# Linear attention twice on one core: mask constants and iotas at other steps, four natural tiles in an idle accumulator, half a weight chunk on another queue

## The chip, the cores and the metric

The kernel runs on one core of a Trainium2 chip. The core has five engines with instruction streams of their own, tied together by semaphores only: TensorE (PE in the profile, PEld for its weight loads), VectorE (DVE), ScalarE (ACT), GpSimd (POOL) and SyncE (SP), which here only issues DMAs. The metric is the device time of one execution in microseconds.

## The reference

Two independent linear-attention blocks A and B with the same shapes; their outputs are put side by side.

```python
# for each block: x (1, 2048, 640), wqkv (640, 1920), wo (640, 640), 32 heads of 20
q, k, v = split(x @ wqkv)                            # per head
phi = lambda t: where(t > 0, t + 1, exp(t)) + 1e-6
pq, pk = phi(q), phi(k)
kv  = einsum("bhsd,bhse->bhde", pk, v)               # summed over all 2048 rows
z   = einsum("bhsd->bhd", pk)
o   = einsum("bhqd,bhde->bhqe", pq, kv) / (einsum("bhqd,bhd->bhq", pq, z) + 1e-6)
out = o.reshape(1, 2048, 640) @ wo
```

All in float32.

## The kernel before, in words

**Accuracy.** A float32 product is made of three faster ones: each operand is split into a high part (a rounded copy, line 198, on ACT) and a low part (operand minus high, line 195, on DVE), and the kernel sums high·high, low·high and high·low. A name that ends in h or l is such a part: `wh`, `wl` of a weight chunk, `kah`, `kal` and `ksh`, `ksl` of transposed x, `xnh`, `xnl` of natural x, `pkh`, `pkl` of phi(k).

**Tiling.** x has 32 tiles of 128 rows (16 of A, 16 of B) and 5 chunks of 128 columns. Every tile comes in twice from DRAM: transposed ("t", for k = x·wk) and natural ("n", for the sums). Both go into the five buffers `xr` (`load_x`, line 418), issued on SP.

**Stages.** (1) The head (lines 1106 to 1171): the first three tiles' chunks and the chunks of wk arrive in small DMAs and are split at once; seven dummy matmuls on `psi` run meanwhile. Then `first_chunk` does chunk 0 of tiles 0 to 2, with the left half of the weight chunk's columns first and the right half after it, and the steps ("c", n, c) do chunk c of tile n (`plain`, line 606), up to tile 5. Chunks 0 and 1 of wk use `wh`, `wl`; the later ones use `wfh`, `wfl`. (2) From tile 6 on, k is computed for two tiles at a time by steps ("p", p, product), a Strassen-like form (line 350) with sums of weight blocks (the jobs `f1`, `f2`, lines 866 to 874, on DVE) and sums of x (the jobs `s1` to `s6`, line 459); its parts are added up in `ko` by the jobs `q` (line 357, on DVE). (3) phi in four jobs per tile: `exp`, `relu`, `mix` (line 565), and the split `ph` (line 577, ACT) and `pl` (line 581, DVE). z is summed by an accumulating DMA on POOL's queue (`zs`, `zd<-ek`). (4) The sums G = phi(k)ᵀ·x over groups of four tiles, steps ("H" or "G", group, slice), lines 205 to 207 into `psg`, whose results DVE adds into the accumulator `gacc` of 5 x 640 columns (line 651; the first group is copied, line 649). The jobs `nh` and `nl` split natural x for them. (5) kv from G (line 788), then the denominators, the q products (`psq`) and the output, from about 291 us to the end.

**What sets the order.** The steps of TensorE are listed once, then shifted by the table `MOVED`. Every job of the other engines has a place, a step plus a number from the table `SHIFT`; a job's instructions on all its engines, its DMAs included, are issued at that place. `perform` sorts both lists and issues everything in that order; each engine then runs its own instructions strictly in order. The loads of wk of block B ("ld", "k", 1, c), the stores ("st", pair, part) of split x to DRAM (lines 270 to 274) and the loads of x all share SP's queue.

**Constants.** `constants` makes the three masks used from stage 5 on: three iotas on POOL and six DVE operations (lines 313 to 321), all at step ("c", 4, 2).

Of the kernel before, what the change touches and what calls it, by code (L numbers as in the profile page):

```python
# [14 lines left out]
H = 32  # L15
# [15 lines left out]
    ('fdl', 'k', 1, 4): 4.77, ('fdl', 'k', 1, 8): 1.97, ('fdl', 'm', 0, 1): -0.43, ('fdl', 'm', 0, 2): 1.2, ('fdl',  # L31
# [8 lines left out]
    ('gacc', 0, 3): 0.36, ('gacc', 0, 6): 1.73, ('gacc', 1, 3): 0.64, ('gacc', 1, 5): 1.74, ('gacc', 2, 1): 2.89,  # L40
    ('gacc', 2, 3): 0.28, ('gacc', 3, 0): 0.42, ('gacc', 3, 1): 2.86, ('gacc', 3, 2): 2.99, ('gacc', 3, 3): 3.83,
    ('gacc', 3, 5): 2.14, ('gacc', 3, 6): 1.96, ('gacc', 4, 0): 0.75, ('gacc', 4, 4): 2.17, ('gacc', 4, 5): 4.46,
    ('gacc', 5, 0): 0.6, ('gacc', 5, 3): 1.28, ('gacc', 5, 5): 0.51, ('gacc', 5, 6): 1.36, ('gacc', 6, 2): 0.82,
    ('gacc', 6, 4): 0.59, ('gacc', 7, 0): 0.31, ('gacc', 7, 1): 0.04, ('gacc', 7, 2): 2.56, ('gacc', 7, 4): 0.07,
    ('gacc', 7, 5): 0.78, ('gacc', 7, 6): 2.69, ('iota', 0): 0.8, ('kt', 0): 0.53, ('kt', 1): 1.13, ('kt', 5): 4.11,
    ('kvh', 0): 1.2, ('kvh', 1): 5.05, ('kvh', 4): 1.1, ('kvl', 1): 2.02, ('kvl', 3): 2.08, ('kvl', 5): -0.64,
    ('ld', 'k', 1, 1): -0.06, ('ld', 'k', 1, 2): -2.17, ('ld', 'k', 1, 3): -8.75, ('ld', 'k', 1, 4): -3.84, ('ld',
    'm', 0, 0): 1.22, ('ld', 'm', 0, 1): 0.8, ('ld', 'm', 0, 2): 1.54, ('ld', 'm', 0, 3): -0.03, ('ld', 'm', 0, 4):
    -0.19, ('mc', 4, 1): 0.69, ('mix', 0): -0.53, ('mix', 10): 0.15, ('mix', 11): 0.24, ('mix', 12): 0.49, ('mix',
    13): 7.61, ('mix', 14): 4.05, ('mix', 15): 0.17, ('mix', 17): 1.76, ('mix', 19): 1.66, ('mix', 20): 0.31,  # L50
# [87 lines left out]
def tile_linear_attn_pair(ctx: ExitStack, tc: tile.TileContext, ins, out: bass.AP):  # L138
# [171 lines left out]
    def constants():  # L310
        ij = base.tile([P, P], I32, name="ij", tag="kvt", bufs=3)
        nc.gpsimd.iota(ij, pattern=[[1, P]], base=0, channel_multiplier=-1)
# [1275 lines left out]
```

## Time and profile before

| | us |
|---|---|
| runs | 571.79, 572.67, 573.43 (median 572.67) |
| profiled execution | 572.12 |
| its span on the core | 570.3 |
| outside the span | 1.8 |
| PE busy | 564.0 (99%) |
| DVE busy | 438.6 (77%) |
| ACT busy | 334.6 (59%) |
| POOL busy | 84.3 (15%) |

The granted TensorE clock was 1.0 over the span. A timeline row gives start, duration, engine, line, operation, the tile written and the tiles read, and in brackets the idle time of that engine just before and what ended it; "SPq" or "ACTq" is a DMA issue, whose duration is that of issuing. Matmuls overlap in the pipeline, so their spacing is read from start to start.

### The profile page before, as it was taken

The numbers are of one execution on the slowest core, as the hardware profiler recorded it, in microseconds if no ns is written. First come the engines' busy times: TensorE is split into PE (matmuls) and PEld (weight loads), VectorE is DVE, ScalarE is ACT, GpSimd is POOL, SyncE is SP. The second block draws the span as 40 slices with busy tenths as digits, with TensorE's granted clock in tenths as the row PEclk, the third lists the DMA queues.
The fourth block names the chain that finished last, engine by engine and source line by source line (L and its number), as shares of the span: only waits on it lengthen the run. The fifth ranks groups of instructions, "written<-read, shape, count | busy, mean of one in ns | idle before, by whom it ended". The sixth has DMA issues, their size and how long they took to land.

```text
span 570.3 us, 9067 instructions
## 1 busy us (share of the span) xinstructions
PE 564.0 (99%) x3243; PEld 513.8 (90%) x3243; DVE 438.6 (77%) x729; ACT 334.6 (59%) x625; POOL 84.3 (15%) x141
## 2 busy tenths in 40 slices
PE   8999999999999999999999999999999999999997
PEld 6989989898999898989888899898989989898997
DVE  6888698886584878788745799977798786768792
ACT  6863667664575775656736665746556464644551
POOL 0121132411011212143100103220012201001010
PEclk9999999999999999999999999999999999999999
DMA  8777689999985786998998977762455994122022
GB/s 285 192 206 201 180 208 333 269 326 363 340 185 130 190 238 114 376 236 260 334 273 279 328 231 251 260 193 95 131 197 170 393 366 140 48 66 92 1 93 92
DMA packets 71700, 123.58 MB, mean 217 GB/s; under 512 B 9000, under 2 KB 33960, under 8 KB 71656
## 3 DMA queue, kind: packets, MB, share of 16 engines
q1 hardware_dynamic: 59352, 83.29, 44.7%
q0 software_dynamic: 12160, 39.66, 25.1%
q8 instruction: 25, 0.41, 0.3%
q14 instruction: 19, 0.16, 0.1%
q10 hardware_dynamic: 144, 0.07, 0.0%
HBM read 73.62 MB, written 49.37 MB: 216 GB/s over the span
## 4 chain that ended last, share of the span: by engine, by line
PE 89%; DVE 5%; DMA 4%; issue 1%; ACT 1%; SPq 0%; POOL 0%; POOLq 0%; DVEq 0%; ACTq 0%
PE pa L350 21%; PE pe L350 11%; PE psq L205 8%; PE psq L207 8%; PE psq L206 8%; PE psg L206 7%; PE psg L207 7%; PE psg L205 7%; PE psb L350 6%; PE pskv L788 2%; PE psk L606 2%; DMA wst<-in_B_wk 1%; DMA zd<-ek 1%; DVE xnl L195 1%; DMA x<-in_A_xt_tiles 1%
## 5 line engine op out<-in xcount | busy, mean ns | idle before, releaser
L205 PE MATMUL psq<-xqh,wqh 128*128 128x512 f32 x200 | 78.4, 392 | 0.0
L207 PE MATMUL psq<-xqh,wql 128*128 128x512 f32 x200 | 78.0, 390 | 0.0
L206 PE MATMUL psq<-xql,wqh 128*128 128x512 f32 x200 | 77.9, 389 | 0.0
L207 PE MATMUL psg<-pkh,xnl 128*128 128x512 f32 x160 | 62.8, 392 | 0.3 <-DVE xnl L195 0.3
L206 PE MATMUL psg<-pkl,xnh 128*128 128x512 f32 x160 | 62.8, 393 | 0.0
L205 PE MATMUL psg<-pkh,xnh 128*128 128x512 f32 x160 | 62.8, 393 | 0.0
L354 ACT ACTIVATE o<-pa 128x320 f32<-128x320 f32 x64 | 27.9, 439 | 45.8 <-PE pa L350 45.6
L958 DVE SCALAR_TENSOR_TENSOR pq<-eq,rq 128x512 f32<-128x512 f32 x40 | 27.6, 690 | 27.7 <-ACT rq L957 27.7
L573 POOL DMA_DIRECT2D zd<-ek x30 | 26.1, 870 | 136.1 <-DVE ek L565 59.9
L207 PEld LDWEIGHTS psq<-xqh,wql 128*128 128x128 f32 x200 | 37.5, 188 | 7.9
L956 ACT ACTIVATE eq<-psq 128x512 f32<-128x512 f32 x40 | 23.9, 597 | 34.9 <-PE psq L207 32.6
L354 ACT ACTIVATE ko<-pa 128x320 f32<-128x320 f32 x52 | 22.5, 434 | 37.3 <-PE pa L350 37.1
L206 PEld LDWEIGHTS psq<-xql,wqh 128*128 128x128 f32 x200 | 37.6, 188 | 7.2
L205 PEld LDWEIGHTS psq<-xqh,wqh 128*128 128x128 f32 x200 | 37.6, 188 | 7.2
L207 PEld LDWEIGHTS psg<-pkh,xnl 128*128 128x128 f32 x160 | 30.0, 188 | 7.0 <-DVE xnl L195 0.7
L206 PEld LDWEIGHTS psg<-pkl,xnh 128*128 128x128 f32 x160 | 30.0, 188 | 6.3 <-DVE pkl L581 1.0
L205 PEld LDWEIGHTS psg<-pkh,xnh 128*128 128x128 f32 x160 | 30.1, 188 | 5.3 <-DVE kvt L795 0.2
L577 ACT ACTIVATE pkh<-ek,epst 128x640 fp32r<-128x640 f32 x32 | 26.3, 831 | 8.4 <-DVE ek L565 8.3
L651 DVE TENSOR_TENSOR gacc<-psg,gacc 128x512 f32<-128x512 f32 (+2 forms) x42 | 26.0, 628 | 6.2 <-PE psg L207 5.9
L581 DVE SCALAR_TENSOR_TENSOR pkl<-ek,pkh 128x640 fp32r<-128x640 f32 x32 | 26.0, 820 | 5.2 <-ACT pkh L577 5.2
L195 DVE TENSOR_TENSOR xnl<-xn,xnh 128x640 fp32r<-128x640 f32 x32 | 25.8, 818 | 5.4 <-ACT xnh L485 5.1
L565 DVE SCALAR_TENSOR_TENSOR ek<-ek,ko 128x640 f32<-128x640 f32 x32 | 26.2, 820 | 4.6 <-ACT ko L562 3.3
(208 smaller groups left out, 1679.5 us busy)
## 6 DMA issues: line engine op xcount, KB each, us to landing
zd<-ek POOLq DMA_DIRECT2D x32, 320.0 KB, 5.7
out<-o POOLq DMA_DIRECT2D x28, 320.0 KB, 3.9
xql<-xd SPq DMA_DIRECT2D x24, 256.0 KB, 4.0
xn<-in_A_x SPq DMA_DIRECT2D x16, 320.0 KB, 5.5
xt<-in_B_xt_tiles SPq DMA_DIRECT2D x16, 320.0 KB, 5.3
xn<-in_B_x SPq DMA_DIRECT2D x16, 320.0 KB, 5.6
xqs<-in_A_xt SPq DMA_DIRECT2D x20, 256.0 KB, 6.3
xqs<-in_B_xt SPq DMA_DIRECT2D x20, 256.0 KB, 4.2
```

The lines of the kernel that those rows point to most:

```text
L195: nc.vector.tensor_tensor(lo, src, f32(hi), op=OP.subtract)
L205: nc.tensor.matmul(o, whi, xhi, start=first, stop=False)
L206: nc.tensor.matmul(o, whi, xlo, start=False, stop=False)
L207: nc.tensor.matmul(o, wlo, xhi, start=False, stop=last)
L350: nc.tensor.matmul(o, x, y, start=start and m == r == 0, stop=m == len(terms) - 1 and r == 2, skip_group_check=True)
L354: nc.scalar.activation(x, y, AF.Copy)
L565: nc.vector.scalar_tensor_tensor(ek[n], ek[n], 1.0, rk[n], op0=OP.min, op1=OP.add)
L573: nc.gpsimd.dma_start(zacc[b], e, accum_op=OP.add)
L577: nc.scalar.activation(pk[n][0], ek[n], AF.Identity, bias=epst)
L581: nc.vector.scalar_tensor_tensor(lo, ek[n], EPS, f32(hi), op0=OP.add, op1=OP.subtract)
L651: nc.vector.tensor_tensor(o, x, o, op=OP.add)
L958: nc.vector.scalar_tensor_tensor(pq[u][:, c, :], e, 1.0, r, op0=OP.min, op1=OP.add)
```

## The change

Four edits, and both tables have other numbers.

1. `constants` is cut in two. The three iotas (`counts`) stand at ("p", 3, 0), the six DVE operations at ("p", 4, 5); before, all stood at ("c", 4, 2). The iotas' three buffers are held in between.
2. Natural x of tiles 0 to 3 is loaded into `gacc[0][:, n]`, the accumulator of block A, which holds nothing until the first group's sums are copied into it. Those four loads no longer take an `xr` buffer.
3. The right half of wk's chunk 0 is issued from ACT's queue, right after its x load, and no longer from SP behind x of tiles 1 and 2.
4. Chunk 1 of tiles 0 to 2: the products with the weight's high part are done for all three tiles first, and the products with its low part after them.

```diff
@@ load_x
-        x = xr[kind, n] = kx[0].tile([P, D], F32, name=f"x{kind}", tag="xr", bufs=5)
+        if kind == "n" and n < 4:
+            if n == 0:
+                gacc[0] = base.tile([P, NC, D], F32, name="gacc", tag="gacc", bufs=1)
+            x = xr[kind, n] = gacc[0][:, n]
+        else:
+            x = xr[kind, n] = kx[0].tile([P, D], F32, name=f"x{kind}", tag="xr", bufs=5)
@@ plain
-        for i, j in ((0, 0), (1, 0), (0, 1)):
+        for i, j in ((0, 0), (1, 0), (0, 1))[2 * (c == 1 and n in first):]:
@@ head
     nc.sync.dma_start(t[:, :HF], ins[0]["wk"][:P, :HF])
+    nc.scalar.dma_start(t[:, HF:], ins[0]["wk"][:P, HF:])
     part(1, 0, 3)
-    nc.sync.dma_start(t[:, HF:], ins[0]["wk"][:P, HF:])
@@ first_chunk, at its end
+        for n in first:
+            for i in range(2):
+                for h in range(2):
+                    plain_mm(n, 1, i, 0, h)
@@ jobs
-    job(("constants",), ("c", 4, 2), constants)
+    job(("counts",), ("p", 3, 0), counts)
+    job(("constants",), ("p", 4, 5), constants, after=[("counts",)])
@@ SHIFT, one entry of many
-    ('nl', 0): 0.1, ('nl', 1): 2.6,
+    ('nl', 0): -0.75,
```

The lines behind the table stand up to 20 lower in the changed kernel (line 195 is 177 there, 606 is 598).

TensorE in chunk 1 of tiles 0, 1, 2 (its weight parts are `wh`, `wl`; x of tile 0 is `kah`, `kal`, of tile 1 `ksh`, `ksl`, of tile 2 again `kah`, `kal`; x2 are the two column halves). Before:

```order
L606 MATMUL psk<-wh,kah 128x320 x2
L606 MATMUL psk<-wh,kal 128x320 x2
L606 MATMUL psk<-wl,kah 128x320 x2
L606 MATMUL psk<-wh,ksh 128x320 x2
L606 MATMUL psk<-wh,ksl 128x320 x2
L606 MATMUL psk<-wl,ksh 128x320 x2
```

After:

```order
L598 MATMUL psk<-wh,kah 128x320 x2
L598 MATMUL psk<-wh,kal 128x320 x2
L598 MATMUL psk<-wh,ksh 128x320 x2
L598 MATMUL psk<-wh,ksl 128x320 x2
L598 MATMUL psk<-wh,kah 128x320 x2
L598 MATMUL psk<-wh,kal 128x320 x2
L598 MATMUL psk<-wl,kah 128x320 x2
```

The first matmul that reads `wl` stood behind four others of the chunk and now stands behind twelve.

VectorE at the first sums (28 to 35 us before): `pkl` and `xnl` are the low parts that the sums read, `ek<-ek,ko` is `mix`, `ij`, `same` and `mask` are the constants. Before:

```order
L581 SCALAR_TENSOR_TENSOR pkl<-ek,pkh 128x640
L313 TENSOR_SCALAR ij<-ij 128x128
L314 TENSOR_SCALAR same<-ij 128x128
L320 TENSOR_SCALAR mask_438<-v_437 128x120
L321 SCALAR_TENSOR_TENSOR mask_438<-v_437,mask_438 128x120
L320 TENSOR_SCALAR mask_443<-v_442 128x80
L321 SCALAR_TENSOR_TENSOR mask_443<-v_442,mask_443 128x80
L565 SCALAR_TENSOR_TENSOR ek<-ek,ko 128x640
L195 TENSOR_TENSOR wfl_448<-t_267,wfh_447 128x320
L195 TENSOR_TENSOR xnl<-xn,xnh 128x640 x2
L581 SCALAR_TENSOR_TENSOR pkl<-ek,pkh 128x640
```

After (the `xnl<-gacc` are those of tiles 1, 2 and, in the last row, 3):

```order
L177 TENSOR_TENSOR xnl<-gacc,xnh 128x640 x2
L177 TENSOR_TENSOR kal<-xt,kah 128x128
L858 TENSOR_TENSOR t_398<-wst 128x320
L859 TENSOR_TENSOR wst<-wst 128x320
L177 TENSOR_TENSOR ksl<-xt,ksh 128x256
L865 TENSOR_TENSOR t_398<-wst 128x320
L866 TENSOR_TENSOR t_422<-wst,t_398 128x320
L177 TENSOR_TENSOR wfl_418<-t_259,wfh_417 128x320
L557 SCALAR_TENSOR_TENSOR ek<-ek,ko 128x640
L573 SCALAR_TENSOR_TENSOR pkl<-ek,pkh 128x640 x2
L177 TENSOR_TENSOR xnl<-gacc,xnh 128x640
```

The constants are gone from here, and `xnl` of tile 1, which stood behind them beside that of tile 3, now stands nine rows ahead of the last `pkl`.

VectorE in the second group's sums (66 us on before), behind the two `pkl` of tiles 6 and 7: `t` and `wst` are block sums of wk (`f1`), `sx` sums of x, `gacc` the additions. Before:

```order
L581 SCALAR_TENSOR_TENSOR pkl<-ek,pkh 128x640 x2
L459 TENSOR_TENSOR sx<-xt 128x256
L459 TENSOR_TENSOR sx<-sx,xt 128x256
L866 TENSOR_TENSOR t_909<-wst 128x320
L867 TENSOR_TENSOR wst<-wst 128x320
L565 SCALAR_TENSOR_TENSOR ek<-ek,ko 128x640
L651 TENSOR_TENSOR gacc<-psg,gacc 128x512
```

After:

```order
L573 SCALAR_TENSOR_TENSOR pkl<-ek,pkh 128x640 x2
L302 TENSOR_SCALAR ij<-ij 128x128
L303 TENSOR_SCALAR same<-ij 128x128
L307 TENSOR_SCALAR mask_884<-ij 128x120
L308 SCALAR_TENSOR_TENSOR mask_884<-ij,mask_884 128x120
L307 TENSOR_SCALAR mask_887<-ij 128x80
L308 SCALAR_TENSOR_TENSOR mask_887<-ij,mask_887 128x80
L858 TENSOR_TENSOR t_890<-wst 128x320
L859 TENSOR_TENSOR wst<-wst 128x320
L451 TENSOR_TENSOR sx<-xt 128x256
L451 TENSOR_TENSOR sx<-sx,xt 128x256
```

The six operations of the constants stand here now, ahead of the block sums of wk and of the second group's `gacc` additions.

More of the change, by code (lines that the diff above doesn't have):

```diff
@@ L19 @@
 SHIFT = {
[3 rows of a table removed]
-    6): 1.78, ('c5', 8): 1.02, ('constants',): 1.46, ('exp', 0): 2.17, ('exp', 10): 0.04, ('exp', 11): 0.73, ('exp',
-    13): 3.23, ('exp', 14): 0.41, ('exp', 15): 0.95, ('exp', 16): 0.91, ('exp', 18): -0.02, ('exp', 20): -0.96,
-    ('exp', 22): 1.7, ('exp', 25): 0.96, ('exp', 28): 1.07, ('exp', 29): 0.86, ('exp', 3): 4.78, ('exp', 4): 0.2,
[5 rows of a table removed]
-    ('fdl', 'k', 1, 4): 4.77, ('fdl', 'k', 1, 8): 1.97, ('fdl', 'm', 0, 1): -0.43, ('fdl', 'm', 0, 2): 1.2, ('fdl',
[8 rows of a table removed]
-    ('gacc', 0, 3): 0.36, ('gacc', 0, 6): 1.73, ('gacc', 1, 3): 0.64, ('gacc', 1, 5): 1.74, ('gacc', 2, 1): 2.89,
@@ L41 @@
[L41 to L50, printed above, removed]
@@ L51 @@
-    ('mix', 23): 0.53, ('mix', 24): -0.1, ('mix', 26): 0.21, ('mix', 29): 2.2, ('mix', 3): -0.55, ('mix', 4): 7.31,
[20 rows of a table removed]
-    ('relu', 1): 0.33, ('relu', 10): 1.37, ('relu', 11): 0.09, ('relu', 13): 1.06, ('relu', 14): 1.59, ('relu', 17):
-    0.14, ('relu', 2): 0.27, ('relu', 21): 4.46, ('relu', 25): 2.55, ('relu', 28): 1.48, ('relu', 30): 3.49,
[19 rows of a table removed]
-    1.07, ('woh', 4): -0.51, ('wol', 0): 0.5, ('wol', 3): 0.03, ('wol', 4): 0.03, ('wqh', 1): 2.01, ('wqh', 3):
[2 rows of a table removed]
[3 rows of a table added]
+    0): 2.55, ('exp', 11): 0.74, ('exp', 13): 3.23, ('exp', 14): 0.41, ('exp', 15): 0.95, ('exp', 16): 0.91, ('exp',
@@ new lines @@
+    18): -0.02, ('exp', 20): -0.96, ('exp', 22): 1.7, ('exp', 25): 0.96, ('exp', 28): 1.07, ('exp', 29): 0.86,
+    ('exp', 3): 4.78, ('exp', 4): 0.16, ('exp', 5): 2.09, ('exp', 6): 0.87, ('exp', 8): -0.31, ('exp', 9): 2.13,
+    ('f1', 'k', 0, 1): 0.31, ('f1', 'k', 1, 0): -0.71, ('f1', 'm', 0, 0): 1.2, ('f1', 'm', 0, 1): -0.83, ('f2', 'k',
+    0, 1): 2.5, ('f2', 'm', 0, 0): 0.42, ('f5', 'k', 0): -0.1, ('f5', 'k', 1): -2.28, ('fdh', 'k', 1, 2): 0.51,
+    ('fdh', 'k', 1, 4): 0.91, ('fdh', 'k', 1, 6): 0.53, ('fdh', 'k', 1, 8): 3.31, ('fdh', 'm', 0, 6): 0.52, ('fdh',
[8 rows of a table added]
@@ new lines @@
+    ('gacc', 0, 1): 3.2, ('gacc', 0, 4): 1.75, ('gacc', 1, 0): 2.35, ('gacc', 1, 3): 2.05, ('gacc', 2, 1): 2.89,
+    ('gacc', 2, 3): 0.28, ('gacc', 3, 1): 2.86, ('gacc', 3, 2): 2.86, ('gacc', 3, 3): 3.83, ('gacc', 3, 5): 2.14,
+    ('gacc', 4, 0): 0.75, ('gacc', 4, 4): 2.17, ('gacc', 5, 0): 0.6, ('gacc', 5, 3): 1.28, ('gacc', 5, 5): 0.51,
+    ('gacc', 6, 2): 0.82, ('gacc', 6, 4): 0.59, ('gacc', 7, 0): 0.31, ('gacc', 7, 1): 0.04, ('gacc', 7, 4): 0.45,
+    ('gacc', 7, 5): 1.7, ('gacc', 7, 6): 2.69, ('iota', 0): 0.8, ('kt', 0): 0.53, ('kt', 1): 1.13, ('kt', 5): 5.23,
@@ new lines @@
+    ('kvh', 0): 1.2, ('kvh', 1): 5.9, ('kvh', 4): 1.1, ('kvl', 1): 2.02, ('kvl', 3): 2.08, ('kvl', 5): -0.64, ('ld',
+    'k', 1, 0): 0.56, ('ld', 'k', 1, 1): -0.06, ('ld', 'k', 1, 3): -9.42, ('ld', 'k', 1, 4): -3.84, ('ld', 'm', 0,
+    0): 1.22, ('ld', 'm', 0, 1): 0.8, ('ld', 'm', 0, 2): 1.54, ('ld', 'm', 0, 3): -0.03, ('ld', 'm', 0, 4): -0.19,
+    ('mc', 4, 1): 0.69, ('mix', 11): 0.24, ('mix', 12): 0.49, ('mix', 13): 7.61, ('mix', 14): 4.05, ('mix', 15):
+    -0.8, ('mix', 17): 1.76, ('mix', 19): 1.66, ('mix', 2): -0.07, ('mix', 20): 0.31, ('mix', 23): 0.53, ('mix',
@@ L96 @@
+    24): -0.1, ('mix', 26): 0.21, ('mix', 29): 2.2, ('mix', 3): -0.55, ('mix', 4): 7.31, ('mix', 5): 7.49, ('mix',
[18 rows of a table added]
+    1.37, ('relu', 11): 0.09, ('relu', 13): 1.06, ('relu', 14): 1.59, ('relu', 17): 0.14, ('relu', 21): 4.46,
+    ('relu', 25): 2.55, ('relu', 28): 1.48, ('relu', 30): 3.49, ('relu', 5): 1.82, ('s1', 10): -0.46, ('s1', 12):
[17 rows of a table added]
     -0.99, ('xh', 12, 'A1'): 1.16, ('xh', 12, 'A2'): -3.99, ('xh', 12, 'A5'): -0.04, ('xh', 12, 'S1'): 1.16, ('xh',
     13, 'S1'): 0.74, ('xh', 14, 'A1'): -8.23, ('xh', 14, 'A5'): 1.32, ('xh', 15, 'A2'): 2.54, ('xh', 15, 'A5'):
[21 rows of a table removed]
[16 rows of a table added]
@@ L308, in tile_linear_attn_pair, with counts @@
     nc.vector.memset(epst, EPS)
+    def counts():
+        for n in (P, 6 * DH, 4 * DH):
+            mask[n] = base.tile([P, n], I32 if n == P else F32, name="ij", tag="kvt", bufs=3)
+        nc.gpsimd.iota(mask[P], pattern=[[1, P]], base=0, channel_multiplier=-1)
+        for nh in (6, 4):
+            nc.gpsimd.iota(mask[DH * nh], pattern=[[0, DH], [-DH, nh]], base=0, channel_multiplier=1,
+                           allow_small_or_imprecise_dtypes=True)
     def constants():
-        ij = base.tile([P, P], I32, name="ij", tag="kvt", bufs=3)
-        nc.gpsimd.iota(ij, pattern=[[1, P]], base=0, channel_multiplier=-1)
+        ij = mask.pop(P)
         nc.vector.tensor_scalar(ij, ij, H - 1, None, op0=OP.bitwise_and)
@@ L315, in constants @@
         for nh in (6, 4):
-            v = base.tile([P, DH * nh], F32, name=f"v{nh}", tag="kvt", bufs=3)
+            v = mask.pop(DH * nh)
             m = base.tile([P, DH * nh], F32, name=f"mask{nh}")
-            nc.gpsimd.iota(v, pattern=[[0, DH], [-DH, nh]], base=0, channel_multiplier=1,
-                           allow_small_or_imprecise_dtypes=True)
             nc.vector.tensor_scalar(m, v, 0.0, None, op0=OP.is_ge)
```

148 rows, old and new, of tables (MOVED, SHIFT) are left out of this document.

## The prediction

> **What bounds the kernel.** I read the page first.
>
> ```profile
> span 570.3 us, 9067 instructions
> PE 564.0 (99%) x3243; PEld 513.8 (90%) x3243; DVE 438.6 (77%) x729; ACT 334.6 (59%) x625; POOL 84.3 (15%) x141
> ```
>
> TensorE is busy for 564.0 of 570.3 us, and the change neither adds nor drops a matmul. So only 6.3 us can be had at all, 1.0 of them ahead of the first dummy matmul; a loss has no such limit. The time moves by what is done to PE's few stalls and by new ones. The view of waits for PE names the old ones:
>
> ```profile
> PE psi L1103 <- DVE idle L1100: 1.0, 1, 1.0
> PE psk L606 <- DVE wl L195: 0.6, 1, 0.6
> PE pa L350 <- ACT mev L354: 0.5, 1, 0.5
> PE psg L207 <- DVE xnl L195: 0.3, 1, 0.3
> PE psg L207 <- DVE pkl L581: 0.2, 1, 0.2
> PE pe L350 <- DVE ko L357: 0.2, 1, 0.2
> ```
>
> These are idle times. A stall costs more, since matmuls overlap and the first one behind a stall takes longer; so I price stalls from start to start.
>
> **The head**, in the timeline:
>
> ```profile
> 0.74 0.40 ACTq L1112 DMA_DIRECT2D x<-in_A_xt_tiles  x1
> 1.65 0.46 SPq L1139 DMA_DIRECT2D wst<-in_A_wk  x1
> 3.28 0.47 ACT L198 ACTIVATE wh<-wst 128x320 fp32r<-128x320 f32 x1 [0.82 <-DMA wst<-in_A_wk]
> 3.69 0.31 ACT L198 ACTIVATE ksh<-x 128x128 fp32r<-128x128 f32 x1
> 5.27 0.31 PE L606 MATMUL psk<-wh,kah 128*128 128x320 f32 x1
> 5.33 0.47 ACT L198 ACTIVATE wh<-wst 128x320 fp32r<-128x320 f32 x1 [1.13 <-DMA wst<-in_A_wk]
> 7.16 0.31 ACT L198 ACTIVATE kah<-x 128x128 fp32r<-128x128 f32 x1 [0.20 <-DMA x<-in_A_xt_tiles]
> 8.12 0.82 DVE L195 TENSOR_TENSOR wl<-wst,wh 128x640 fp32r<-128x640 f32 x1
> 8.99 0.56 PE L606 MATMUL psk<-wl,kah 128*128 128x320 f32 x2 [0.58 <-DVE wl L195]
> 9.39 0.46 PE L606 MATMUL psk<-wh,ksh 128*128 128x320 f32 x2
> 11.15 0.45 PE L606 MATMUL psk<-wfh,kah 128*128 128x320 f32 x2
> ```
>
> From 9.39 to 11.15 PE starts 12 matmuls, unhindered, 0.147 us each. From 5.27 to 11.15 it starts 30 (12 left of chunk 0, 18 of chunk 1), which at that pace are 4.41 us and take 5.88: 1.47 us are lost here, to three arrivals: the second half of the weight chunk, x of chunk 1, and `wl`. Everything behind 1.65 on SP (wk's chunk 1, x of chunk 1) is queued behind that half.
>
> **The first sums**, from the timelines of DVE, PE and SP:
>
> ```profile
> 28.05 0.82 DVE L581 SCALAR_TENSOR_TENSOR pkl<-ek,pkh 128x640 fp32r<-128x640 f32 x1
> 30.41 0.52 DVE L313 TENSOR_SCALAR ij<-ij 128x128 int32<-128x128 int32 x1 [1.55 <-POOL ij L312]
> 31.95 0.82 DVE L565 SCALAR_TENSOR_TENSOR ek<-ek,ko 128x640 f32<-128x640 f32 x1
> 33.09 1.56 DVE L195 TENSOR_TENSOR xnl<-xn,xnh 128x640 fp32r<-128x640 f32 x2
> 34.56 0.82 DVE L581 SCALAR_TENSOR_TENSOR pkl<-ek,pkh 128x640 fp32r<-128x640 f32 x1
> 33.26 0.40 PE L206 MATMUL psg<-pkl,xnh 128*128 128x512 f32 x1
> 33.96 0.50 PE L207 MATMUL psg<-pkh,xnl 128*128 128x512 f32 x1 [0.30 <-DVE xnl L195]
> 35.43 0.50 PE L206 MATMUL psg<-pkl,xnh 128*128 128x512 f32 x1
> 36.00 0.39 PE L205 MATMUL psg<-pkh,xnh 128*128 128x512 f32 x1
> 74.73 0.39 PE L206 MATMUL psg<-pkl,xnh 128*128 128x512 f32 x1
> 79.72 0.39 PE L207 MATMUL psg<-pkh,xnl 128*128 128x512 f32 x1
> 15.71 8.17 SPq L418 DMA_DIRECT2D xn<-in_A_x  x2
> ```
>
> DVE stands 1.55 us for the iotas, spends 1.54 (30.41 to 31.95) on the constants, and then does `xnl` and `pkl` just as PE wants them. PE starts eight 512-column matmuls from 33.26 to 36.00, 2.74 us; unhindered, from 74.73 to 79.72, it starts 22 in 4.99 us, 0.227 each, so eight are 1.82: 0.9 us lost. SP's row is the wait of natural x for a free `xr` buffer.
>
> **The change, part by part.**
>
> *Weight half on ACT's queue and the new order of chunk 1.* ACT's issue costs what its neighbour does, 0.40 us, in front of an ACT that stands 0.82 us before `wh` at 3.28: hidden, with 0.4 left; without that cover the first matmul would come 0.4 later. SP's queue loses one issue of 0.46 us, so chunk 1's transfers are issued half a microsecond earlier. `wl` is wanted 12 matmuls into the chunk and not 4: 8 x 0.147 = 1.2 us more slack. It cost 0.58 idle and a slow restart (8.99 to 9.39 is 0.40 for two matmuls, not 0.29), 0.7 together; that stall goes whatever the DMAs do. For PE to run on without a gap, the half must land 0.1 to 0.2 us earlier (it is wanted three matmuls behind 5.27, at 5.71, and its `wh` ends at 5.80), and x of chunk 1 half a microsecond earlier (`kah` is wanted 12 matmuls behind 5.27, at 7.03, and ends at 7.47). Both are about what the issue alone gives. Bounds: 0.7 us (the `wl` stall alone) to 1.47; I take 1.3, nearest to the sum of the three stalls, since two of them need only that half microsecond. How the transfer itself goes is shown by the bandwidth, in the windows view (last two numbers: busy share of the DMA engines, GB/s):
>
> ```profile
> 2.80:3.20 0.40, 0.40 (x3) 0.12 (x2) 0.00 (x0) 0.00 (x0) 0.00 (x0) 1.00 1.05 310
> 3.20:3.60 0.40, 0.40 (x3) 0.09 (x1) 0.11 (x1) 0.32 (x1) 0.00 (x0) 1.00 0.54 76
> ```
>
> The engines drop from 310 to 76 GB/s while the half has been issued for a microsecond: they were not full, and a second queue can use the hole. Against this speaks the Trainium skill, DMA: Bandwidth & Descriptors, section Issuing engines are not separate DMA queues: DMAs of all issuing engines run on the same 16 engines and interleave, and several issuers save only the issue time. By that rule the transfer of chunk 1 would gain the issue time and no more, and the total would be 0.5 us less good (rival a); the 76 GB/s row says that there was room, so I lean to the row.
>
> *Natural x in the accumulator.* Four loads stop waiting for `xr`; they are issued several microseconds ahead of 15.71 to 23.88, and transposed x finds four more buffer turns. The accumulator's first copy comes behind the last `xnl`, as before behind the first sums, so no new wait. Alone it moves no PE row: 0, because `pkl`, not the load, is last at 35.43. If the earlier bytes delayed a weight chunk by their time, up to 0.5 us would be lost.
>
> *Constants away from here.* 1.55 + 1.54 = 3.1 us of DVE are freed ahead of `xnl` and `pkl`, and the two stalls there are 0.9 together, so both go: 0.9. The other bound is 0, if another wait of DVE took the place of that for the iotas; I know of none.
>
> *Constants at ("p", 4, 5).* The iotas are long done there, so no wait, but 1.54 us of DVE come in front of block sums and `gacc` additions. The rows of that place, of DVE, SP and PE:
>
> ```profile
> 66.39 1.56 DVE L581 SCALAR_TENSOR_TENSOR pkl<-ek,pkh 128x640 fp32r<-128x640 f32 x2 [0.23 <-ACT pkh L577]
> 90.01 0.49 DVE L866 TENSOR_TENSOR t<-wst 128x320 f32<-128x320 f32 x1 [1.45 <-DMA wst<-in_B_wk]
> 81.54 0.94 SPq L235 DMA_DIRECT2D wst<-in_B_wk  x1
> 93.55 0.41 PE L350 MATMUL pe<-wfh,ksh 128*128 128x320 f32 x1 [0.23 <-DVE ko L357]
> ```
>
> From 66.39 DVE runs nearly without a pause until it stands 1.45 us for the load issued at 81.54, and that delay ends in PE's wait at 93.55. PE arrives in this stage 2.2 us earlier (1.3 + 0.9); DVE, behind the constants, only 0.7. The sums wait in three `psg` buffers for DVE, nine or twelve matmuls of 0.227 each, 2 us and more, so 1.54 us of lateness is mostly under them: 0 to 1.5, I take 0.1, nearest to the three buffers. What is late next is SP: the load stands in its queue behind stores of x parts that DVE has just split. If it is issued 1.8 us earlier, 8.4 us from issue to landing as now, PE has 2.2 and loses 0.4 more than today. Bounds: 0.4 gained (today's stall gone) to 2.2 + 1.5 = 3.7 lost (the load later by the constants' whole time); I take 0.4 lost, because in the changed order one store and the splits of that pair stand further ahead of the load than now.
>
> *Tables.* At 131 us:
>
> ```profile
> 129.46 0.74 ACT L553 ACTIVATE ek<-ko 128x640 f32<-128x640 f32 x1 [2.11 <-DMA zd<-ek]
> 130.10 0.81 ACT L577 ACTIVATE pkh<-ek,epst 128x640 fp32r<-128x640 f32 x1
> 130.95 0.82 DVE L581 SCALAR_TENSOR_TENSOR pkl<-ek,pkh 128x640 fp32r<-128x640 f32 x1 [1.65 <-ACT pkh L577]
> ```
>
> In the changed order that `pkh` stands ahead of the `exp` that stood 2.11 us for a DMA; `pkl` comes 0.64 earlier (129.46 to 130.10), and PE wanted it 0.2 earlier (the view of waits): with a restart 0.4 gained (0 to 0.5). The remaining moves up to 290 us exchange neighbours on engines with idle time; a 0.5 us wait for `mev` stays, as its rows are unchanged. From 290 us on the orders are the same: 0. Each unseen swap could cost or give a few tenths; I take 0 and 0.4 to both sides.
>
> Sum: -1.3 - 0.9 + 0.1 + 0.4 - 0.4 = -2.1 us. The profiled execution, 572.12, becomes 570.0; it stands 0.55 below the median, which becomes 570.6, 0.37% less. 0.3% (1.7 us) is about what a measurement can tell from no change, so this is near the edge.
>
> **Rivals.** (a) *The weight half shares the engines with x of tiles 1 and 2* (this is what the cited rule would do here). `ksh` at 3.69 stands right behind `wh`, and x of tile 1 may be just in time; no row gives its landing. If the half takes turns with it, `ksh` comes later and stalls chunk 0, and chunk 1 gains only what the issue saves. The head gives 0.8, the `wl` stall and little more: total -1.6, 571.1. For it: one set of engines. Against it: 76 GB/s.
>
> (b) *The load for 93.55 gives the lead back.* If it lands 0 to 0.5 us earlier than now, whatever was won ahead is lost there, and only the 0.4 at 131 stays: total -0.4 to -0.9, about 572.0. For it: DVE's 1.45 us wait for just this DMA. Against it: its own queue neighbours were gated by DVE and x loads that come earlier.
>
> (c) *The same place turns slower.* From the point at which the load lands more than 0.4 us later than now, the kernel is slower. The constants in front of the splits, 1.54 us, and none of the lead passed on would make +1.5 - 0.4 = +1.1: 573.8. For it: SP's queue is strictly in order. Against it: DVE enters this stage 2.2 us earlier, more than the constants take.
>
> **How the numbers follow.** Forecast 0.50, (a) 0.18, (b) 0.19, (c) 0.13. Faster by over 0.3%: nine tenths of the forecast and half of (a), 0.54. Slower: (c) without its mildest part, 0.12. Between: 0.34. The range runs from 569.2 (the lost 0.4 at 93.55 gone, its stall too, and the head at 1.47) to 572.9, which holds (b) and leaves out most of (c).
>
> **What would show it.** Right: no PE wait for `wl`, `xnl` or the `pkl` at 131; PE starts chunk 2 near 9.8 and not 11.15; DVE's first constant without idle time before it, near 65 us; the load of 81.54 issued before 80. Wrong: PE waits for `ksh` in chunk 0, for a `psg` buffer near 75, or longer than 0.7 us for `ko` near 91.

## The result, and the profile after

| | before | changed |
|---|---|---|
| median of 10 runs each | 572.77 us | 570.72 us |
| lowest and highest | 571.51 to 574.25 | 569.51 to 571.78 |
| profiled execution, and its span | 572.12, 570.3 | 570.56, 568.8 |

The ratio is 0.9964, with a 95% interval of 0.9950 to 0.9979: 2.05 us faster. A second set of runs of the changed kernel gave 570.68 us, 0.9957 (0.9942 to 0.9973). The two profiled executions differ by 1.6 us only, and, as the experiments show, the place of a stall in one execution is partly a matter of chance. So the steps below are read from many executions. Every ratio is taken against runs of the kernel before made beside it, whose medians lie between 572.53 and 573.14, so times of different experiments are compared by their ratios.

The page of the changed kernel, and the view of waits for PE:

```profile
span 568.8 us, 9069 instructions
PE 563.0 (99%) x3243; PEld 514.4 (90%) x3243; DVE 438.5 (77%) x729; ACT 335.0 (59%) x625; POOL 84.5 (15%) x141
PE psi L1095 <- DVE idle L1092: 1.0, 1, 1.0
PE pa L337 <- ACT mev L341: 1.0, 1, 1.0
PE pa L337 <- ACT ko L341: 0.5, 2, 0.2
```

PE's waits for `wl`, `xnl`, the `pkl` at 131 us and the `ko` of DVE are gone. The wait for `mev`, 0.5 before, is now 1.0, and two waits for `ko` from ACT are new. In this execution, then, stalls were removed early and part of the lead was spent later.

**The head** of the changed kernel, in the timelines of ACT, PE and SP, and one row of its windows view (last two numbers: busy share of the DMA engines, GB/s):

```profile
1.66 0.46 SPq L217 DMA_DIRECT2D wst<-in_A_wk  x1
3.47 0.47 ACT L180 ACTIVATE wh<-wst 128x320 fp32r<-128x320 f32 x1 [0.52 <-DMA wst<-in_A_wk]
4.21 0.31 ACT L180 ACTIVATE ksh<-x 128x128 fp32r<-128x128 f32 x1 [0.27 <-DMA x<-in_A_xt_tiles]
4.62 0.46 ACT L180 ACTIVATE wh<-wst 128x320 fp32r<-128x320 f32 x1
6.41 0.74 ACT L180 ACTIVATE wh<-wst 128x640 fp32r<-128x640 f32 x1 [1.33 <-DMA wst<-in_A_wk]
7.16 0.31 ACT L180 ACTIVATE kah<-x 128x128 fp32r<-128x128 f32 x1
5.85 0.31 PE L598 MATMUL psk<-wh,kah 128*128 128x320 f32 x1
10.30 0.45 PE L598 MATMUL psk<-wfh,kah 128*128 128x320 f32 x2
3.20:3.60 0.40, 0.40 (x3) 0.09 (x1) 0.00 (x0) 0.13 (x1) 0.00 (x0) 1.00 1.22 385
```

Chunk 2 starts at 10.30 and not 11.15, 0.85 earlier. But the way there is not the predicted one. The right half's `wh` runs at 4.62, without a wait for its DMA (before: 5.33, after a wait of 1.13), so the half did land earlier, by 0.7 us or more. The DMA engines moved 385 GB/s from 3.2 to 3.6 us, where they had moved 76. x of tile 1 landed later: ACT waits 0.27 us for it at 4.21, and PE's matmul of 5.27 is at 5.85. Wk's chunk 1 was issued half a microsecond earlier (1.66) and its `wh` still begins at 6.41, before at 6.22; `kah` begins at 7.16 in both. So the whole 0.85 comes from behind 7.16: no wait for `wl`.

**The first sums**, DVE and PE:

```profile
30.43 0.82 DVE L573 SCALAR_TENSOR_TENSOR pkl<-ek,pkh 128x640 fp32r<-128x640 f32 x1 [0.38 <-ACT pkh L569]
31.17 0.82 DVE L177 TENSOR_TENSOR xnl<-gacc,xnh 128x640 fp32r<-128x640 f32 x1
31.51 0.39 PE L187 MATMUL psg<-pkh,xnh 128*128 128x512 f32 x1
34.27 0.39 PE L187 MATMUL psg<-pkh,xnh 128*128 128x512 f32 x1
```

Twelve matmuls start from 31.51 to 34.27, 0.23 us each: no stall is left here.

**The second group's sums, and 91 to 96 us**, DVE, SP and PE:

```profile
65.98 0.22 DVE L302 TENSOR_SCALAR ij<-ij 128x128 int32<-128x128 int32 x1
67.21 0.48 DVE L858 TENSOR_TENSOR t<-wst 128x320 f32<-128x320 f32 x1
79.14 0.80 SPq L217 DMA_DIRECT2D wst<-in_B_wk  x1
86.73 0.49 DVE L858 TENSOR_TENSOR t<-wst 128x320 f32<-128x320 f32 x1
91.56 0.41 PE L337 MATMUL pe<-wfh,ksh 128*128 128x320 f32 x1
95.66 0.41 PE L337 MATMUL pa<-wfh,ksh 128*128 128x320 f32 x1 [0.24 <-ACT ko L341]
```

The constants take 1.23 us of DVE (65.98 to 67.21) without a wait in front. The load that was issued at 81.54 is issued at 79.14, and `f1` begins with it at 86.73, before at 90.01. The wait for `ko` at 93.55 is gone at 91.56; a new one of 0.24 us of idle stands four microseconds further.

**197 us and after**, POOL, ACT and PE. Before:

```profile
191.61 0.93 POOL L573 DMA_DIRECT2D zd<-ek  x1 [5.32 <-DVE ek L565]
192.40 0.76 POOL L856 DMA_DIRECT2D md<-mev  x1
198.83 0.76 ACT L354 ACTIVATE mev<-psm 80x320 f32<-80x320 f32 x2 [2.78 <-PE pa L350]
199.32 0.42 PE L350 MATMUL pa<-wfh,kah 128*128 128x320 f32 x1 [0.50 <-ACT mev L354]
```

Changed:

```profile
190.03 0.95 POOL L565 DMA_DIRECT2D zd<-ek  x1 [5.92 <-DVE ek L557]
190.68 0.92 POOL L848 DMA_DIRECT2D md<-mev  x1
197.12 0.76 ACT L341 ACTIVATE mev<-psm 80x320 f32<-80x320 f32 x2 [3.25 <-DMA md<-mev]
197.61 0.41 PE L337 MATMUL pa<-wfh,kah 128*128 128x320 f32 x1 [0.98 <-ACT mev L341]
233.79 0.42 PE L337 MATMUL pa<-wfh,ksh 128*128 128x320 f32 x1 [0.24 <-ACT ko L341]
```

ACT's copy into a `mev` buffer waits until the DMA `md<-mev` has landed (the view of before names PE as the releaser, but there too the store's landing, at 198.73, came last). From its issue to ACT's going on it takes 6.4 us in both profiles. The issue itself moved from 192.40 to 190.68, 1.7 us, while PE's lead had grown to 2.2: on POOL's queue the store stands behind `zd<-ek`, which waits for DVE and went out only 1.6 us earlier.

To follow where a lead is won and lost, the start of the matmul with the same number in TensorE's order (the same matmul except in a few stretches, the first of them chunk 1) is compared with the profile of before. Negative is earlier, in us; the columns are places of the kernel before. Each row is one execution, the ratio is of the medians: the profiled execution of "old order of chunk 1" was the fastest of its ten (569.48, median 571.32), that of "constants early" a late one (573.05, median 571.00). All rows share the one profile of before, which ran 0.65 us under its median, with chunk 1's weight early (`wh` at 6.22, against 6.60 in the mean).

| kernel | 9.2 | 36.0 | 94.0 | 97.5 | 133 | 200 | 236 | median ratio |
|---|---|---|---|---|---|---|---|---|
| changed | -0.84 | -1.73 | -2.00 | -1.47 | -2.19 | -1.70 | -1.57 | 0.9964 |
| changed, second profile | -0.08 | -0.96 | -0.97 | -0.46 | -0.75 | -0.63 | -0.83 | 0.9957 |
| weight half from SP | -0.21 | -1.09 | -1.60 | -1.13 | -1.88 | -1.38 | -1.76 | 0.9952 |
| old order of chunk 1 | -0.42 | -1.30 | -1.81 | -1.59 | -2.31 | -2.46 | -2.60 | 0.9973 |
| natural x in xr | -0.28 | -1.15 | -1.66 | -1.53 | -2.28 | -2.23 | -2.58 | 0.9960 |
| constants early | +0.14 | +1.45 | +0.95 | +1.19 | +0.44 | +0.41 | +0.83 | 0.9971 |
| before + new order | -0.58 | -0.59 | -0.08 | -0.08 | -0.05 | -0.29 | -0.58 | 1.0017 |
| before + constants moved | -0.11 | -1.01 | +0.28 | +0.28 | +0.31 | -0.06 | +0.66 | 1.0004 |
| before + new tables | +0.16 | +1.54 | +1.48 | +2.00 | +1.28 | +1.13 | +2.75 | 1.0021 |
| changed, old tables | +0.09 | -0.80 | -0.36 | -0.36 | -0.16 | -0.42 | -0.18 | 0.9990 |
| same, one load earlier | -0.22 | -1.09 | -1.41 | -1.41 | -0.88 | -0.25 | -0.57 | 0.9984 |
| changed, md store first | -1.20 | -2.07 | -2.58 | -2.57 | -3.32 | -4.09 | -2.96 | 0.9968 |
| same, weight half from SP | -0.96 | -1.84 | -1.74 | -1.22 | -1.74 | -2.56 | -1.18 | 0.9968 |

### The profile page after: what moved, and what is told of

It is laid out like the page before. It is cut to its first block, busy times and chain, and to the rows that moved or that the text cites. A ratio compares the mean times of both kernels' runs of the same rounds, so it can differ in the third digit from the quotient of the medians.

```text
span 568.8 us, 9069 instructions
## 1 busy us (share of the span) xinstructions
PE 563.0 (99%) x3243; PEld 514.4 (90%) x3243; DVE 438.5 (77%) x729; ACT 335.0 (59%) x625; POOL 84.5 (15%) x141
## 4 chain that ended last, share of the span: by engine, by line
PE 58%; DMA 2%; issue 1%; ACT 0%; DVE 0%; POOL 0%; SPq 0%; DVEq 0%; POOLq 0%
PE pa L337 14%; PE psq L187 8%; PE psq L189 8%; PE psq L188 8%; PE pe L337 7%; PE psb L337 4%; PE psg L188 2%; PE psg L189 2%; PE psg L187 2%; DMA wst<-md 1%; PE pskv L780 1%; DMA md<-mev 1%; PE psd L971 0%; PE psd L970 0%; PE psm L187 0%
## 5 line engine op out<-in xcount | busy, mean ns | idle before, releaser
L180 ACT ACTIVATE dah<-pq 128x1024 fp32r<-128x1024 f32 (+5 forms) x27 | 18.2, 710 | 19.2 <-DVE pq L982 19.2
```

## The experiments

Intervals of the ratios are 0.1 to 0.25 percentage points to both sides, so parts of a few tenths of a microsecond are read from the profiles, and only where they repeat.

### The weight half from SP's queue again

```diff
     nc.sync.dma_start(t[:, :HF], ins[0]["wk"][:P, :HF])
-    nc.scalar.dma_start(t[:, HF:], ins[0]["wk"][:P, HF:])
     part(1, 0, 3)
+    nc.sync.dma_start(t[:, HF:], ins[0]["wk"][:P, HF:])
```

> The changed kernel with the right half of wk's chunk 0 issued from SP again, behind x of tiles 1 and 2. The marker is the start of chunk 2's first matmul (wfh): 11.15 us before, 10.30 in the changed kernel. Theory A (the prediction's sum): the second queue gives the transfer about half a microsecond, so without it chunk 1 starts later and the marker goes to 10.75 or later, the time up by 0.5 us. Theory B (rival a of the prediction: one set of DMA engines, the half only takes turns with x of tiles 1 and 2 and with wk's chunk 1): x of chunk 1 lands when it did, chunk 0 gets its 0.56 us back, the 0.25 us stall in front of the right half's matmuls and the 0.35 us wait for kah return, and the marker stays at 10.2 to 10.4, the time within 0.2 us.

Measured 570.29 us, 0.9952 (0.9938 to 0.9967): the time is no worse, as theory B said. Its marker, though, is 10.94 and not 10.2 to 10.4. The rows of ACT and PE:

```profile
3.91 0.31 ACT L180 ACTIVATE ksh<-x 128x128 fp32r<-128x128 f32 x1
7.17 0.74 ACT L180 ACTIVATE wh<-wst 128x640 fp32r<-128x640 f32 x1 [0.99 <-DMA wst<-in_A_wk]
10.94 0.45 PE L598 MATMUL psk<-wfh,kah 128*128 128x320 f32 x2
```

No wait for x of tile 1, and chunk 1's weight landed late, at 7.17. That landing proved to vary by itself. Over the profiles of all kernels, ACT's `wh` of chunk 1 begins at 6.41, 5.96, 7.51, 7.10, 7.46, 7.16, 5.38 and 7.29 with the half on ACT's queue (mean 6.78), and at 6.22, 7.17, 6.79, 6.42, 6.57 and 6.42 with it on SP's (mean 6.60). So the marker of one execution decided nothing, and the means show no gain of chunk 1 from the second queue. What does repeat: with the half on ACT's queue ACT waits for x of tile 1 in all eight, 0.27 to 0.64 us; on SP's queue in none of six. And the room that the prediction read from its 76 GB/s row was there: from 3.2 to 3.6 us the engines move 351 to 385 GB/s in the eight and 76 to 136 in the six. From 4.4 to 5.2 us it is 243 to 327 GB/s against 248 to 343, so the head start of the half was not passed on to chunk 1; why not stays open.

### Old order of chunk 1

```diff
-        for i, j in ((0, 0), (1, 0), (0, 1))[2 * (c == 1 and n in first):]:
+        for i, j in ((0, 0), (1, 0), (0, 1)):
```

and the added loop at the end of `first_chunk` is gone.

> The changed kernel with chunk 1 of tiles 0 to 2 in the old order, tile by tile, wl products third. Theory B (the head's whole gain is the new order): PE waits for wl again, whose subtraction ends at 8.94 as in both kernels, and chunk 2 starts at 11.1 to 11.2 and not 10.30; the profiled span grows by 0.85 us. Theory A (part of the gain is the second queue): the marker comes to 10.6 to 10.8, a loss of 0.3 to 0.5 us.

Measured 571.32 us, 0.9973 (0.9957 to 0.9989); marker 10.73. By the letter that is theory A's number, but weight chunk 1's `wh` began at 5.96 in this execution, 0.45 before that of the changed kernel. Counted from it, the marker is 4.77 us behind, where the changed kernel has 3.89. This is the measure that the next run was built on. For this execution it misleads, as the rows of DVE and PE show:

```profile
7.54 0.82 DVE L177 TENSOR_TENSOR wl<-wst,wh 128x640 fp32r<-128x640 f32 x1
8.68 0.46 PE L598 MATMUL psk<-wl,kah 128*128 128x320 f32 x2
```

`wl` was ready at 8.36, before PE wanted it at 8.68, and PE's matmuls start 0.15 us apart all the way from 6.77 to the marker. Chunk 1's weight was early and chunk 0, behind x of tile 1, was late, so the old order cost nothing here. It costs only where `wl` is the later one; the time, 0.9973 against 0.9964, doesn't tell the two orders apart.

### The new order alone, in the kernel before

The reverse of the edit above, in the kernel before.

> The kernel before with the new order of chunk 1 alone. The profiles so far show that the landing of wk's chunk 1 moves by more than a microsecond between executions (ACT starts its wh between 5.96 and 7.51), so the start of chunk 2 is counted from there: 4.77 and 4.93 us behind that wh in the old order, 3.73 to 3.89 in the new one. Theory (the head's gain is the order alone): 3.7 to 3.9 behind it here, whatever the landing, and x of tile 1 not waited for by ACT near 3.7. Rival (it takes the second queue too): 4.3 or more. Either way the stalls between 31 and 36 us stay, 0.6 to 1.0 us in all.

```profile
6.79 0.74 ACT L198 ACTIVATE wh<-wst 128x640 fp32r<-128x640 f32 x1 [0.37 <-DMA wst<-in_A_wk]
10.56 0.46 PE L606 MATMUL psk<-wfh,kah 128*128 128x320 f32 x2
```

3.77 us, as the theory said. Over all profiles the new order gives 3.77 (eight times, with the half on either queue), 3.89 and once 4.56, where the weight came at 5.38 and PE, without a gap from 5.25 on, had chunk 0 still to do; the old order gives 4.62, 4.74 and 4.93 in the three profiles in which PE waits for `wl` (0.57 to 0.58 us of idle each), all with the half on SP's queue. So the order gains about 1.0 us counted from the landing, where `wl` is late. But the time did not follow: 573.86 us, 1.0017 (0.9992 to 1.0042), with runs from 570.8 to 577.7. In the table its lead of 0.58 is 0.08 at 94 us, where PE waits 0.7 us for `ko` and not 0.2.

### Constants early again

```diff
-    job(("counts",), ("p", 3, 0), counts)
-    job(("constants",), ("p", 4, 5), constants, after=[("counts",)])
+    job(("counts",), ("c", 4, 2), counts)            # both with the shift 1.46 of before
+    job(("constants",), ("c", 4, 2), constants, after=[("counts",)])
```

> The changed kernel with iotas and constants back at step (c, 4, 2) and the old shift of 1.46 for them. Theory 1 (the prediction: the constants and their wait for the iotas are what made xnl and pkl late at 34 us): DVE stands 1 us or more for the iotas and PE loses 0.4 to 0.9 us between 31 and 35 us. Rival (the other order of xnl, moved ahead by the tables, removed the stalls): PE loses under 0.15 us there. In the second group's sums either gives DVE 1.2 us back, and the 1.2 us wait of DVE near 88 us grows by as much, so nothing is gained there.

POOL, DVE and PE:

```profile
31.01 0.87 POOL L566 DMA_DIRECT2D zd<-ek  x1 [6.63 <-DMA zd<-ek]
32.25 0.52 DVE L303 TENSOR_SCALAR ij<-ij 128x128 int32<-128x128 int32 x1 [2.69 <-POOL ij L296]
35.40 0.50 PE L189 MATMUL psg<-pkl,xnh 128*128 128x512 f32 x1 [1.12 <-DVE pkl L574]
```

Theory 1, and worse than before: the iotas stand on POOL behind an accumulating DMA that waits for the one ahead of it, DVE stands 2.69 us for them, and `pkl` comes 1.12 us late. In the table the loss between 9.2 and 36 us is 1.3 us, against a gain of 0.89 in the changed kernel, a difference of 2.2. The time is 571.0 us, 0.9971 (0.9952 to 0.9990), with runs from 569.5 to 573.8: the median is hardly above the changed kernel, the spread is twice as wide. The profiled execution was one of the late ones (573.05), and five of the ten runs took under 570.3 us; whether the iotas wait as long in those no profile shows.

### Constants moved, in the kernel before

The same two lines of the changed kernel, and its `counts`, in the kernel before.

> The kernel before with the constants alone moved: iotas at (p, 3, 0), the DVE operations at (p, 4, 5). Theory (the wait for the iotas and the constants make xnl and pkl late): PE loses under 0.1 us between 31 and 36 us, where before it lost 0.9. Rival (xnl stands too late in the old order anyway): 0.4 or more stays. In the second group's sums the six operations take 1.2 to 1.5 us of DVE and PE shows no stall between 60 and 90 us by the theory; the rival c of the prediction would show a wait for psg or ko of 0.5 us or more up to 94 us beyond the 0.5 of before.

No stall between 31 and 36 us, 0.90 gained there: the theory. Then SP, DVE and PE at 80 to 94 us:

```profile
80.83 1.42 SPq L235 DMA_DIRECT2D wst<-in_B_wk  x1
90.29 0.49 DVE L871 TENSOR_TENSOR t<-wst 128x320 f32<-128x320 f32 x1 [2.04 <-DMA xt<-in_A_xt_tiles]
93.83 0.41 PE L355 MATMUL pe<-wfh,ksh 128*128 128x320 f32 x1 [1.45 <-DVE ko L362]
```

PE came 1.0 us earlier and the load went out 0.7 us earlier, but it took 9.4 us to land and not 8.4, and `f1` began 0.3 later than before (the view names a load of x there; the one of wk, at 90.20, landed last). PE waits 1.45 us. So this edit alone is what rivals b and c of the prediction described: 572.69 us, 1.0004 (0.9990 to 1.0019), nothing gained.

### Natural x in xr again

```diff
-        if kind == "n" and n < 4:
-            ...
-            x = xr[kind, n] = gacc[0][:, n]
-        else:
-            x = xr[kind, n] = kx[0].tile([P, D], F32, name=f"x{kind}", tag="xr", bufs=5)
+        x = xr[kind, n] = kx[0].tile([P, D], F32, name=f"x{kind}", tag="xr", bufs=5)
```

> The changed kernel with natural x of tiles 0 to 3 in xr buffers again. The prediction's theory: where the loads lie costs nothing by itself, the first sums start at the same time to 0.2 us. Rival: the new order asks for xnl of tiles 1 and 2 and 3 earlier than the xr buffers let their loads be issued (the fourth was issued at 23.5 us before), so ACT and DVE stand for natural x, and PE loses 0.5 us or more between 25 and 36 us.

569.86 us, 0.9960 (0.9937 to 0.9983), and a gain of 0.87 us between 9.2 and 36 us, as in the changed kernel (0.89): by itself the place of those loads costs and gives nothing that shows.

### Old tables in the changed kernel, and the new tables alone

In the first, all four edits with the old `SHIFT` and `MOVED`; in the second, the kernel before with the new ones.

> The changed kernel with the old SHIFT and MOVED tables (its constants and iotas at their new steps, without a shift). Theory: the four edits carry the gain, the span is 568 to 570 us; at 131 us pkh stands behind the exp that waits for a DMA again, and PE loses 0.3 to 0.5 there if that DMA is as late as before. Rival (the tables are what gains): the span is 570 or more, with new waits before 100 us.

572.00 us, 0.9990 (0.9979 to 1.0001), and a span of 570.3 us, the rival's by its number. The four edits without the tables keep a quarter of the gain at most, and the interval reaches no gain at all: the 0.89 at the first sums is there, half of it is gone at 94 us (PE waits 0.60 us for `ko` at 93.19), most of the rest by 133.

> The kernel before with the new tables alone (constants at (c, 4, 2), now without a shift). Theory: the tables alone give at most 0.5 us, at 131 us, and the stalls for the constants between 31 and 36 us stay or grow to 2 us, as they did when the constants were put back into the changed kernel; no gain over before, 571 to 574 us. Rival (the tables carry the gain): 571 us or less.

573.46 us, 1.0021 (1.0011 to 1.0031): the tables alone are slower. Their order puts the iotas further back on POOL, DVE stands 2.75 us for them, and PE loses 1.4 us by 36 us. So neither half carries the gain; they need each other. Which of the four edits the tables need, the times do not show: without any one of them the ratio is 0.9952 to 0.9973, and each interval overlaps that of the changed kernel. The new tables with the constants alone moved were not run, so whether these two carry the gain is not shown.

### One load two stores earlier, with the old tables

```diff
-    ('ld', 'k', 1, 1): -0.06,
+    ('ld', 'k', 1, 1): -3.06,
```

> The changed kernel with the old tables, and in them one number other: the load of wk of B, chunk 1, stands two stores earlier in SP's queue, right behind the two natural loads. With the old tables it was issued at 80.6 to 81.5 us however early PE came, DVE began f1 with it at 89.7 to 90.3, and PE waited 0.6 to 1.5 us for ko at 93. Theory (the lead is handed back at this load, and the tables keep it by issuing it two microseconds earlier): issued near 79, f1 begins before 88.5, PE waits 0.2 us or less for ko near 93. Rival (DVE and the splits are late by themselves): the wait stays 0.5 or more.

SP, DVE and PE:

```profile
78.90 0.49 SPq L235 DMA_DIRECT2D wst<-in_B_wk  x1
88.09 0.47 DVE L876 TENSOR_TENSOR t<-wst 128x320 f32<-128x320 f32 x1
92.14 0.41 PE L355 MATMUL pe<-wfh,ksh 128*128 128x320 f32 x1
130.09 0.44 PE L205 MATMUL psg<-xnh,pkh 128*128 128x384 f32 x1 [0.50 <-ACT pkh L587]
130.96 0.44 PE L207 MATMUL psg<-xnh,pkl 128*128 128x384 f32 x1 [0.24 <-DVE pkl L591]
PE pa L355 <- ACT mev L359: 1.1, 1, 1.1
```

The theory held at its place: with one number of the table changed, the lead of 1.09 is no longer halved but grows to 1.41 at 94 us. Then 0.5 are lost at 130 us and 0.6 at `mev`, and of the lead 0.25 is left at 200 us; 571.78 us, 0.9984 (0.9975 to 0.9993). The two waits at 130 are where the new tables put `pkh` ahead of an `exp`.

### The md store first, and that with the half on SP

```diff
-    ('zs', 20): 0.85,
+    ('zs', 20): 3.0,
```

> The changed kernel with one number of the table other: on POOL's queue the store md<-mev issued at 190.68 goes ahead of the accumulating DMA zd<-ek issued at 190.03, whose place it took behind. ACT's mev at 197.12 waited 3.25 us for an md store to land, and PE 1.0 us behind it. Theory (that landing is what ends the wait): the store is issued near 190.1, lands 0.6 us or more earlier, PE waits 0.5 us or less there; of that at most 0.6 us reaches the end, 570.2 us or so. Rival (PE's wait is for something else, or the next chain, md loaded again near 231 us, takes it back): the end moves by under 0.2 us.

POOL, ACT and PE:

```profile
189.08 0.60 POOL L848 DMA_DIRECT2D md<-mev  x1 [6.11 <-ACT mev L341]
194.36 0.76 ACT L341 ACTIVATE mev<-psm 80x320 f32<-80x320 f32 x2 [1.62 <-DMA md<-mev]
205.32 0.74 ACT L477 ACTIVATE xnh<-xn 128x640 fp32r<-128x640 f32 x1 [1.44 <-DMA xn<-in_B_x]
208.56 0.41 PE L337 MATMUL pa<-wfh,kah 128*128 128x320 f32 x1 [1.05 <-ACT ko L341]
```

PE's wait for `mev` is gone, and the lead at 200 us is 4.09, the largest of all. Eleven microseconds later ACT stands 1.44 us for a load of natural x, and PE waits 1.05 behind it. 570.68 us, 0.9968 (0.9956 to 0.9979): the same as the changed kernel. So the landing does end the wait, as the theory said, and the time is the rival's. In the profile another chain takes 1.1 us back, though not the one that the rival named.

> The changed kernel with the weight half from SP's queue again and the md store first: both single edits that seemed no worse. Theory (the second queue gives nothing, the store 0.3 to 0.6 us): 569.7 to 570.3 us, at or under the changed kernel of the same call. Rival (the second queue was worth half a microsecond): 570.5 or more.

571.01 us, 0.9968 (0.9955 to 0.9980): the theory's 569.7 to 570.3 missed, and no better than the changed kernel. The number is the rival's, but not by its reason, since the half from SP's queue was no slower by itself. What the profile shows is the next chain again: the lead of 2.56 at 200 us is 1.18 at 236, and PE waits 1.33 us for `ko` at 210, behind an ACT that stood 1.71 us for natural x.

### The changed kernel once more

> The changed kernel once more, to see what of its profile repeats. By what the others showed: ACT waits 0.25 to 0.6 us for x of tile 1 near 4.2 us, chunk 2 starts 3.7 to 3.9 us behind the start of chunk 1's wh, whatever that is, no stall between 31 and 36 us, none over 0.2 us at 91.5; the waits for mev at 197 and ko at 234 differ by some tenths from the first profile. Median 570.7, within 0.5 us.

570.68 us, and most points came: ACT waits 0.36 us for x of tile 1, chunk 2 starts 3.77 us behind `wh`, no stall at 31 to 36 us, and 0.62 us for `mev`. The waits for `ko` differ: 0.23 at 92.57, where the first profile has none, 0.25 at 96.67 as in the first, and none near 234. The head, with the weight at 7.29, gave a lead of 0.08 where the first profile had 0.84. So a single profile's head is a draw from a range of more than a microsecond, in a kernel whose median repeats to 0.04 us.

## Why the prediction was right or wrong

The time came out as forecast (570.72 for 570.6). Of the two largest terms the first sums came as forecast and the head by one of its two mechanisms; the other terms were wrong in opposite directions.

- **The head, 1.3 us.** The order of chunk 1 is right and was priced too low: 0.7 for `wl` by the sum, 1.0 by the profiles in which `wl` is late, counted from the landing. The other half of the term failed: that issuing chunk 1's transfers half a microsecond earlier lands them as much earlier. Its `wh` begins at 6.78 us in the mean against 6.60. The 76 GB/s row was read rightly as room, and the half filled it; the step that failed is that this room would also bring chunk 1 forward. Rival a was nearer: x of tiles 1 and 2 comes later, and wk's chunk 1 no earlier, not even by the issue time. The rule cited there (the Trainium skill, DMA: Bandwidth & Descriptors, section Issuing engines are not separate DMA queues) says that transfers of all issuers interleave on the same engines and that a second issuer saves only issue time. The runs agree with the first part (ACT's 0.27 to 0.64 us of waiting for x of tile 1) and not with the second: the half gained 0.7 us or more for an issue 0.47 us earlier (1.18 for 1.65), and chunk 1 gained nothing.
- **The first sums, 0.9 us.** Right, in size too, in the profiles: 0.89, with the constants as the cause, shown by taking them away from the kernel before (0.90) and by putting them back into the changed one (2.2). In time it is not shown: moving them alone gave 1.0004, and putting them back 0.9971 where the changed kernel has 0.9964.
- **Natural x in the accumulator, 0.** Right as far as the profile shows.
- **Constants in the second group's sums, 0.1 lost, and the load behind 93.55, 0.4 lost.** The first is nothing. The second has the wrong sign: with the new tables the load goes out 2.4 us earlier, not 1.8, `f1` begins with it 7.6 us after the issue, not 8.4, PE's lead there is 1.7, not 2.2, and PE gains 0.27 where 0.4 was to be lost. The step that failed is the reading of SP's order: the splits and stores ahead of the load come earlier by the new tables, where with the old ones the changed kernel still issues it at 81.03. Rivals b and c named the right place; they are what happens with the old tables.
- **131 us, 0.4 gained.** About right: 0.55, and it does need the tables; with the old ones the changed kernel loses 0.4 there.
- **"A 0.5 us wait for `mev` stays, as its rows are unchanged"**, and nothing from there to 290 us. Wrong in this profile. The step that failed is that an unchanged row keeps its wait: the rows around it moved by different amounts. ACT wrote the copies that the store reads 2.18 us earlier, as PE's lead of 2.19 has it, but the store went out only 1.72 earlier, behind `zd<-ek`, and 0.49 was lost at 197 us. With the store first the wait was gone. The loss is no fixed one: with leads of 2.3 at 133 us the profiles of the old order and of natural x in `xr` lose next to nothing there, as their stores took 5.9 and 6.1 us and not 6.4. At 234 another 0.49 was lost, in this profile alone of the changed kernel's two, and not in those of the half from SP, the old order and natural x. Between them 0.36 came back, from small stalls at 211 and 215 us that did not return. Near 95.66 another 0.52 was lost, also unforeseen; this belongs to the new tables, since all nine profiles with them lose 0.0 to 0.5 between 94 and 97.5 us and the four with changes but the old tables nothing.

Added up in the first profile: -0.85, -0.89, -0.27, +0.52, -0.72 (97.5 to 133 us), +0.49, -0.36, +0.49 make -1.6, as the two profiled executions differ. The forecast of -2.1 meets the medians' -2.05, and part of that agreement is luck: the term that failed in the head (0.5 too much) and the three losses that were missed at 95, 197 and 234 us (1.5) stand against 1.4 that were not asked for (0.1 at the second group's sums, 0.7 at the load, 0.3 up to 133 us, 0.4 at 211) and against the 0.5 between the profiles and the medians. That last 0.5 is which executions were profiled: the one of before ran 0.65 under its median, the one of the changed kernel 0.16. The two profiles of the changed kernel end 0.8 and 1.6 us ahead of the one profile of before.

## What to carry to other kernels

A lead on a bound engine is worth only what the next DMA-paced chain lets through: a load queued behind stores, a buffer freed by a store's landing. Price a removed stall together with the next two or three such chains, even where the change does not touch their rows. For a wait whose end is set by a DMA, ask what that DMA's issue waits for: the wait grows by the part of the lead that the issue does not share (0.5 of 2.2 us at `mev`), and then varies with the DMA's own time. Before a stall of some tenths in the first microseconds is explained, look at it in several executions, and count from the landing that starts it rather than from the start of the span, after seeing that the engine did wait for that landing.

## What the runs showed of the hardware that was not expected

- The landing of one and the same 320 KB weight chunk in the first microseconds moves between 5.4 and 7.5 us in eight profiles with the same issues ahead of it, and between 6.2 and 7.2 in the six with the half ahead of it on SP's queue.
- A transfer moved to a second queue came 0.7 us or more earlier itself (its copy begins at 4.62 to 4.87 without a wait for it, against 5.33 to 5.95 after one) and made one on the other queue late, by 0.27 to 0.64 us of waiting, in all eight profiles. The next transfer on that other queue came no earlier (6.78 us in the mean, 6.60 without the move).
- The store `md<-mev`, whose end frees a buffer, took 5.3 and 5.5 us from its issue on POOL until the waiting engine went on where it was issued first (189.08 to 194.36 and 190.61 to 196.12), and 5.8 to 7.0 us in the twelve profiles in which an accumulating DMA was issued just ahead of it (190.68 to 197.12 in the changed kernel).
